# A fused spectral filter and ReGLU layer: the first chunk is split into halves behind an fp32 transpose, the opening list is rewritten, and the inverse pass copies its rows in steps of their own

## The chip, the cores and the metric

The kernel runs on one core of a Trainium2 chip. Its time is the device time of one execution in microseconds (us); the time of before is 449.02 us, the median of three runs (449.0 to 449.44).

## The reference, cut to what matters

```python
def reference(A_x, A_w_r, A_w_i, B_x, B_W_gate, B_W_up, B_W_down):   # x is (1, 2048, 448)
    x = A_x
    xn = _layernorm(x, axis=-1)
    X = rfft2(xn) * (w_r + 1j * w_i)            # over both axes, w is (2048, 225)
    y = irfft2(X)
    gate = xn @ W_gate                          # W_gate and W_up are (448, 1792)
    h = relu(gate) * (xn @ W_up)
    return x + y + h @ W_down                   # W_down is (1792, 448)
```

Both branches start from the same normalized rows and are added to the input.

## The kernel before, in words

Every fp32 operand of a matmul is split into two fp16 halves, a high one and a low one (the rounded value and the remainder), and a product takes three passes: high by high, low by high, high by low. The 2048 rows lie as 16 blocks of 128 rows. Block numbers go by `n2`; the four blocks with the same `n2 % 4` make a **chunk**, and the chunks are worked in the order 0, 2, 1, 3 (`CHUNKS`). A chunk's normalized rows are held transposed in a tile `T` (128 partitions x 8 slices x 512 columns: slices 0 to 3 the high halves of the 448 features, 4 to 6 and a part of 7 the low ones).

The gated branch is the bulk of TensorE's work. A unit `gu` (`gu_full`, L728 to L732) makes gate and up of one group of 128 hidden features for one chunk, in two banks of a PSUM tile `gu` of which there are two buffers. The 448 features don't fill four slices of 128, so the last half slices of two units are packed into four half-height matmuls (`gu_half`, L738) that stand together; the two units that share them are called mates. After a unit ScalarE takes relu of the gate (L768), VectorE multiplies (L772), ScalarE makes the high half (L776) and VectorE the low half (L780); only then is that `gu` buffer free. The down projection `dn` (L799) is added into `xy` by VectorE (L805). Hidden features go in groups of 5, 5 and 4.

The spectral branch runs behind this, as a list of background pieces (`bg`) that the scheduler hands out by a credit: column transforms by matmul (L361, L398, L630, L649), butterflies on VectorE (L404 to L428), the product with the filter (L502 to L505), and exchanges between the upper and the lower 64 partitions by DMA. In the inverse pass an exchange (`i_swap`, L591 to L593) first copies one row of a small tile `row` into partition 64 of the block's tile, which is a DMA issued on SyncE's queue (L592), and then issues two DMAs of 63 partitions into a tile `sw` (L529, L530); `i_pair` (L535, L536) adds the exchanged halves and `i_quad` (L602 to L607) makes sums and differences of the groups. Step numbers in the list `il` (L948) say how many steps after a block's exchange each piece comes: pair and quad stand at 2, `i_hi` at 3.

The first chunk's opening is an order written out by hand (`OPENING`, L30 to L41), one word for each piece, and within one engine the instructions stand in the order of these words. `lx` loads a block, `st` takes its mean and variance on VectorE, `sq` and `rs` make the reciprocal deviation (ScalarE, then four or five small VectorE instructions), `hi` writes the fp16 high half straight from the input on ScalarE (L300), `xn` the fp32 normalized rows on VectorE (L293), `lo` their difference (L317, L318), `cp` copies the odd columns on GpSimd. `tpA` and `tpB` are fp16 transposes on TensorE (L332), three of the high half and five of the rest for each block, into a PSUM tile `fx`, and `ev` copies them to `T` on VectorE (L340) or ScalarE (L338). `wsq`, `par`, `wsc`, `whi`, `wlo` scale and split the gate and up weights of one hidden group; `hh`, `lh`, `hl` are pieces of the first unit, over half of the chunk's columns each (the last digit names the half: 0 is blocks 0 and 4, 1 is blocks 8 and 12). `warm` and `kw1`, `kw3`, `kw6` are 19, 1, 3 and 6 matmuls on a tile of zeros whose result nobody reads (L1049). The later chunks are transposed by DMA (L326).

Of the kernel before, what the change touches and what calls it, by code (L numbers as in the profile page):

```python
# [9 lines left out]
F16 = mybir.dt.float16  # L10
# [20 lines left out]
lx0 lx4 lw lid lw lx8 lx12 lw lw lw lw lx2 lx10 lx6 lx14 lwd0 lwd1 lwd2 lwd3 lwd4 warm st0 st4 sqA rsA hi4  # L31
xn4 xn0 wsqW0g0 cp4 st8 hi0 parW0g0 st12 wsqW0g1 cp0 tpA0 lo0 tpA4 kw1 wscW0g0 sqB tpB0 kw6 parW0g1 wsqW1g0
rsB whiW0g0 vevB0 lo4 wsqW1g1 xn12 tpB4 kw3 hi8 parW1 wscW0g1 xn8 whiW0g1 cp8 vevA0 vevA4 hi12 tpA8 vevB4
hh10 hh00 lo8 wsqW2g1 cp12 tpA12 hl00 lo12 aevA12 tpB8 aevA8 hl10 wloW0g0 lw aevB8 tpB12 wscW1 lh00 aevB12
wloW0g1 lw lfd hh01 hh11 whiW1g0 st2 lh01 lh10 whiW1g1 hl01 wloW1g0 lw hl11 wsqW2g0 wloW1g1 lw ly0 ly4 ly8
ly12 lh11 wsqW3g0 st10 parW2 hp0 st14 wsqW3g1 gu1g0 st6 wdq0 parW3 wscW2 sqC wscW3 whiW2g0 rsC gu1g1 re0
wloW2g0 whiW3g1 tm0 whiW2g1 xn6 wsqW4g0 xn2 gu2g0 wloW2g1 hi2 re1 xn10 gh0 wloW3g1 whiW3g0 tm1 gu2g1 wdq1
wloW3g0 hi10 xn14 lo2 hi14 hi6 cp14 hp2 wsqW4g1 cp2 lo6 gu3g0 cp10 dm2 lo14 re2 parW4 wdq2 cp6 wscW4 tm2
whiW4g0 dm14 lo10 wdq4 gu3g1 wloW4g0 gh1 dm10 gl0 whiW4g1 gl1 dm6 gu4g0 re3 wloW4g1 wdq3 tm3 wdp gh3
wdsc gh2 gu4g1 gl2 wdh1 wdh2 wdl1 wdh0 wdl2 hp4 gl3 re4 wdh3 tm4 wdl0 gh4 wdh4 gl4 wdl3 wdl4  # L40
# [42 lines left out]
def _constants():  # L83
# [55 lines left out]
    ident = np.eye(128, dtype=np.float16)  # L139
# [5 lines left out]
def tile_gfnet_reglu(ctx: ExitStack, tc: tile.TileContext, x, xr, wgu, wd, wf, ident, c_fd, c_fm, c_im, c_row, c_id,  # L145
# [59 lines left out]
    id_t = ft([128, 128], F16, "id_t")  # L205
# [49 lines left out]
    rst = {}  # L255
# [7 lines left out]
    def ln_rstd(q, js=(0, 1, 2, 3), bias=False):  # L263
        w, m = rst[q, js[0]]
        sd, r0, t, r, nm = (w[:, i] for i in range(5))
        V.reciprocal(r0, sd)
        V.scalar_tensor_tensor(t, m[:, :, 1], 1e-5, r0, op0=OP.add, op1=OP.mult)
        V.scalar_tensor_tensor(t, t, -0.5 * 2048, r0, op0=OP.mult, op1=OP.mult)
        V.scalar_tensor_tensor(r, t, 1.5 * 2048, r0, op0=OP.add, op1=OP.mult)
        if bias:  # L270
            V.scalar_tensor_tensor(nm, m[:, :, 0], -1.0, r, op0=OP.mult, op1=OP.mult)
        for i, j in enumerate(js):
            rst[q, j] = r[:, i:i + 1], nm[:, i:i + 1], m[:, i, 0:1]
# [3 lines left out]
    for t in tts:  # L277
        G.memset(t[:, 7, 48:64], 0.0)
    for q in CHUNKS:
        G.memset(Tl[q][32:64], 0.0)  # L280

# [4 lines left out]
    def ln_xn(n2, act=False):  # L286
        xn_b[n2] = free.pop(0)
        xn[n2] = xn_b[n2].rearrange("p g c k -> p (g c k)")[:, 0:D]
        r, nm, mean = rst[n2 % 4, n2 // 4]
# [38 lines left out]
    def ln_tp(n2, tiles):  # L328
        if n2 not in tp:
            tp[n2] = fx().bitcast(F16).rearrange("p (a b) -> p a b", b=128)  # L330
        for a in tiles:
            P.transpose(tp[n2][:, a, :], tt[n2][:, a, :], id_t)  # L332

    def ln_ev(n2, a0, a1, act):
        q, j = n2 % 4, n2 // 4
        o = Tq[q][:, a0:a1, 128 * j:128 * (j + 1)]
        if act:
            last["A"] = A.activation(o, tp[n2][:, a0:a1], AF.Copy).ins  # L338
        else:
            last["V"] = V.tensor_copy(o, tp[n2][:, a0:a1]).ins  # L340


    def t_ninth(q):

        T = Tq[q]
        with tc.issue_after(last.get("R", last["S"])):
            for r in range(3):
                nc.sync.dma_start(Tl[q][16 * r:16 * (r + 1)], T[112:128, 4 + r])
            nc.sync.dma_start(Tl[q][64:128], T[64:128, 3])
# [867 lines left out]
```

## Time and profile before

| what | value |
|---|---|
| median of three runs | 449.02 us |
| profiled execution, its own time | 449.44 us |
| its span, first to last instruction | 447.6 us |
| TensorE busy / VectorE busy / ScalarE busy | 437.9 / 387.2 / 186.7 us |
| granted TensorE clock, mean of the span | 0.998 |

The profiled execution is the slowest of the three, 0.42 us above their median; 1.8 us of it lie outside the span. In a row of the timeline the first number is the start, the second the time from the first start to the last end of a group, and `x6` says how many instructions were merged; the square bracket holds the idle time before the group and what ended it. Matmuls are pipelined: the distance from start to start is what one costs the engine, while its own duration also holds the way through the array.

### The profile page before, as it was taken

Reading aid. Unit: us, or ns where it says so; the run is one execution under the profiler, and the core shown is the slowest. Engines: PE = TensorE matmul, PEld = TensorE weight load, DVE = VectorE, ACT = ScalarE, POOL = GpSimd, SP = SyncE. Lnnn points to the kernel's source line nnn. Section 1 sums busy time; section 2 is a strip of 40 time slices with the busy share of each in tenths; the row PEclk is TensorE's granted clock in tenths of the full one; section 3 lists DMA queues with packets and bytes.
Section 4 is the critical chain, followed back from the end, with each engine's and each line's share of the span. In section 5 each row is a group of like instructions: output and inputs, shape, how many; then the busy total and the mean of one; then the engine's idle time right before and its main releaser. Section 6 shows DMA issues by size and latency. Waiting matters only on the chain.

```text
span 447.6 us, 7353 instructions
## 1 busy us (share of the span) xinstructions
PE 437.9 (98%) x2616; PEld 218.8 (49%) x2616; DVE 387.2 (87%) x958; ACT 186.7 (42%) x398; POOL 28.8 (6%) x77
## 2 busy tenths in 40 slices
PE   6999999999999999999999999999999999999996
PEld 2644645545445444444444444444445555555653
DVE  5999779777969998999999999999789799699753
ACT  5896263742553955133124255344214134134230
POOL 4220020200100140000000000000000000000000
PEclk9999999999999999999999999999999999999999
DMA  7828985400001272412220210001011211211212
GB/s 259 313 68 246 320 334 105 96 0 22 2 1 48 95 243 74 132 54 72 84 84 2 83 41 1 1 1 61 23 41 55 68 34 56 89 34 48 94 63 82
DMA packets 37756, 39.54 MB, mean 88 GB/s; under 512 B 16550, under 2 KB 33624, under 8 KB 37720
## 3 DMA queue, kind: packets, MB, share of 16 engines
q1 hardware_dynamic: 37720, 39.09, 28.0%
q8 instruction: 20, 0.33, 0.3%
q14 instruction: 16, 0.13, 0.1%
HBM read 24.38 MB, written 3.67 MB: 63 GB/s over the span
## 4 chain that ended last, share of the span: by engine, by line
PE 52%; DVE 38%; DMA 3%; issue 3%; ACT 2%; POOL 1%; SPq 1%; DVEq 0%; ACTq 0%; POOLq 0%
PE gu L731 26%; PE dn L799 12%; DVE g L772 3%; DVE h L780 3%; DVE wt L685 3%; DVE xy L805 2%; PE fx L630 2%; PE fx L649 2%; DVE y L502 2%; DVE y L503 2%; DVE y L405 2%; DVE y L404 2%; DMA sw<-y 2%; DVE y L427 2%; PE gu L738 2%
## 5 line engine op out<-in xcount | busy, mean ns | idle before, releaser
L731 PE MATMUL gu<-T,wt 128*128 128x512 f16 (+1 forms) x1140 | 255.0, 375 | 0.0
L731 PEld LDWEIGHTS <-wt 128*128 128x128 f16 x1140 | 108.8, 98 | 128.3 <-issue 8.5
L799 PE MATMUL dn<-wdt,h 128*128 128x448 f16 x624 | 127.1, 352 | 0.3 <-DVE xy L805 0.3
L799 PEld LDWEIGHTS <-h 128*128 128x128 f16 x624 | 60.3, 98 | 57.7 <-issue 1.1
L776 ACT ACTIVATE h<-g 128x512 f16<-128x512 f32 x56 | 35.0, 627 | 78.8 <-DVE g L772 78.6
L768 ACT ACTIVATE g<-gu 128x512 f32<-128x512 f32 x56 | 33.0, 589 | 73.7 <-PE gu L738 52.1
L772 DVE SCALAR_TENSOR_TENSOR g<-gu,g 128x512 f32<-128x512 f32 x56 | 38.2, 682 | 4.2 <-ACT g L768 4.2
L780 DVE TENSOR_TENSOR h<-g,h 128x512 f16<-128x512 f32 x56 | 38.2, 683 | 3.1 <-ACT h L776 2.6
L805 DVE SCALAR_TENSOR_TENSOR xy<-dn,dsc,xy 128x448 f32<-128x448 f32 x44 | 29.8, 678 | 6.2 <-PE dn L799 6.2
L614 ACT ACTIVATE vt<-y,fsc 128x456 f16<-128x456 f32 x16 | 10.8, 672 | 29.9 <-PE fx L630 17.4
L681 ACT ACTIVATE wt<-wst,wsc 128x512 f16<-128x512 f32 x28 | 19.0, 714 | 6.2 <-DVE wsc L196 6.2
L189 POOL PARTITION_ALL_REDUCE wm<-wm x15 | 9.3, 617 | 181.9 <-ACT junk L186 161.8
L654 DVE SCALAR_TENSOR_TENSOR xy<-fx,fsc,xy 128x448 f32<-128x448 f32 x16 | 10.9, 679 | 11.0 <-PE fx L649 10.9
L685 DVE SCALAR_TENSOR_TENSOR wt<-wst,wsc,wt 128x512 f16<-128x512 f32 x28 | 20.2, 744 | 0.1
L738 PE MATMUL gu<-T,wt 64*128 64x512 f16 x112 | 17.0, 381 | 1.6 <-DVE g L772 1.4
L535 DVE TENSOR_TENSOR y<-y,sw 128x228 f32<-128x228 f32 x32 | 12.4, 388 | 6.8 <-DMA sw<-y 4.1
L186 ACT ACTIVATE junk<-wst 128x512 bf16<-128x512 f32 x28 | 17.4, 622 | 1.3 <-DMA wst<-in_wgu 1.0
L405 DVE TENSOR_TENSOR y<-y,y 128x456 f32<-128x456 f32 x22 | 13.8, 628 | 1.7 <-DMA row<-y 1.4
L392 DVE TENSOR_TENSOR Xh<-X,Xh 128x456 f16<-128x456 f32 x16 | 9.9, 626 | 5.8 <-ACT Xh L389 5.7
L404 DVE TENSOR_TENSOR y<-y,y 128x456 f32<-128x456 f32 x22 | 13.8, 628 | 0.4
L630 PE MATMUL fx<-im,vt 128*128 128x128 f16 x192 | 13.5, 219 | 0.0
L389 ACT ACTIVATE Xh<-X 128x456 f16<-128x456 f32 x16 | 9.2, 577 | 10.1 <-DVE X L387 8.9
(128 smaller groups left out, 476.2 us busy)
## 6 DMA issues: line engine op xcount, KB each, us to landing
sw<-y SPq DMA_DIRECT2D x64, 112.2 KB
wst<-in_wgu SPq DMA_DIRECT2D x28, 256.0 KB
wf<-in_wf SPq DMA_DIRECT2D x16, 228.0 KB
y<-in_xr SPq DMA_DIRECT2D x16, 224.0 KB
xy<-in_x SPq DMA_DIRECT2D x16, 224.0 KB
out<-xy SPq DMA_DIRECT2D x15, 224.0 KB
wdst<-in_wd SPq DMA_DIRECT2D x14, 224.0 KB
fm<-in_c_fm SPq DMA_DIRECT2D x4, 256.0 KB
```

What stands on the lines that cost most here:

```text
L404: V.tensor_tensor(t, a, b, op=OP.add)
L405: V.tensor_tensor(b, a, b, op=OP.subtract)
L630: P.matmul(o, v[:, h, w], m[:, c, :], start=(i == 0), stop=(i == 2), skip_group_check=True)
L685: V.scalar_tensor_tensor(w[:, 4:8, :], st, sc, w[:, 0:4, :], op0=OP.mult, op1=OP.subtract)
L731: last["P"] = P.matmul(hps[f, q][:, g, cs], wt[f, g][:, a, :], Tq[q][:, b, cs], start=(start and i == 0), stop=(stop and i == len(seq) - 1 ...
L738: m = P.matmul(hps[f, q][:, g, 0:512], wt[f, g][rows, 7, :], Tq[q][rows, b, :], start=start, stop=not start).ins
L768: last["A"] = A.activation(g1s[f, q], hps[f, q][:, 0, :], AF.Relu, scale=2.0 ** -22).ins
L772: last["V"] = V.scalar_tensor_tensor(g1, hps[f, q][:, 1, :], 2.0 ** -22, g1, op0=OP.mult, op1=OP.mult).ins
L776: A.activation(ht[f, q][:, 0, :], g1s[f, q], AF.Copy)
L780: V.tensor_tensor(h[:, 1, :], g1s.pop((f, q)), h[:, 0, :], op=OP.subtract)
L799: last["P"] = P.matmul(ps[:, 0:D], ht[f, q][:, a, js], wdt[f][:, b, :], start=(i == 0), stop=(i == n - 1)).ins
L805: last["V"] = V.scalar_tensor_tensor(xy[:, n2, :], dps[n2][:, 0:D], dsc[:, g:g + 1], xy[:, n2, :], op0=OP.mult, op1=OP.add).ins
```

## The change

The first chunk is no longer split before it is transposed. `ln_xw` (VectorE) writes the normalized fp32 rows of a block into the memory of its `tt` tile, `ln_xd` (ScalarE) doubles the last 64 columns, and `ln_tp` makes four transposes of 128 x 128 in fp32 with an fp32 identity (64 KB, loaded now from ScalarE's queue). `ln_thi` on ScalarE takes the high half out of PSUM in two instructions (64 rows of the last slice, then all four slices), and `ln_tlo` on VectorE subtracts it from PSUM for the low half, also in two. So 32 fp16 transposes become 16 in fp32, and `hi`, `xn`, `lo`, `cp` and `ev` of this chunk go. GpSimd clears one more piece of 32 x 512 before the tile of zeros is cleared, and the four small clears of `tt` move behind the transposes; `t_ninth` issues three more DMAs for this chunk.

The list `OPENING` is rewritten, with `rs` and `wsc` cut into single steps. The gate and up weights lie in memory with each 256 KB tile in one piece. In the inverse pass the row copy becomes a piece of its own, `i_row`, two steps after the exchange; `i_quad` goes from step 2 to step 3, all later pieces go one step later, and `stage4` is called one pair of blocks ahead, in the forward product too.

```diff
-lx0 lx4 lw lid lw lx8 lx12 lw lw lw lw lx2 lx10 lx6 lx14 lwd0 lwd1 lwd2 lwd3 lwd4 warm st0 st4 sqA rsA hi4
-xn4 xn0 wsqW0g0 cp4 st8 hi0 parW0g0 st12 wsqW0g1 cp0 tpA0 lo0 tpA4 kw1 wscW0g0 sqB tpB0 kw6 parW0g1 wsqW1g0
...
+lx0 lx4 lw st0 lx8 lx12 lw lw lw lwd2 lid lw lw lwd0 st4 lwd1
+lx6 root lx2 sqA lwd3 warm rsA0 rsA1 kw1 rsA2 rsA3 rsA4 wsqW0g0 lwd4 xn0 parW0g0
+xn4 xd0 xd4 tp0 wsqW0g1 tp4 st8 wscW0g0.0 parW0g1 st12 lx10 wscW0g0.1 lx14 sqB kw6 rsB0
+rsB1 wsqW1g0 whiW0g0 rsB2 rsB3 rsB4 tu0 kw3 th0 tu4 xn12 th4 xn8 tl0 tv0 wscW0g1.0
+xd12 wscW0g1.1 tv4 xd8 tl4 wloW0g0 wsqW1g1 hh00 whiW0g1 parW1 tp8 wscW1.0 wsqW2g1 tp12 tu12 lh00
+wloW0g1 wscW1.1 th12 lw hh10 tu8 hl10 tv12 tl12 th8 hl00 tl8 tv8 hh01 ly0 whiW1g1
...
-        eng.dma_start(wst[f, g], wgu[f, :, g])
+        eng.dma_start(wst[f, g], wgu[f, g])
...
-    for t in tts:
-        G.memset(t[:, 7, 48:64], 0.0)
     for q in CHUNKS:
         G.memset(Tl[q][32:64], 0.0)
+    G.memset(Tq[CHUNKS[0]][32:64, 7], 0.0)
...
+    def ln_xw(n2, act=False):
+        r, nm, mean = rn[n2 % 4, n2 // 4]
+        if act:
+            A.activation(xw[n2][:, 0:D], xr_t[n2], AF.Identity, scale=r, bias=nm)
+        else:
+            V.tensor_scalar(xw[n2][:, 0:D], xr_t[n2], mean, r, op0=OP.subtract, op1=OP.mult)
+
+    def ln_xd(n2):
+        A.activation(xw[n2][:, 448:512], xw[n2][:, 384:448], AF.Copy)
+
+    def ln_tp(n2):
+        tp[n2] = fx().rearrange("p (a b) -> p a b", b=128)
+        for a in range(4):
+            P.transpose(tp[n2][:, a, :], xw[n2][:, 128 * a:128 * (a + 1)], id_t)
+        G.memset(tts[n2 // 4][:, 7, 48:64], 0.0)
+
+    def ln_thi(n2, part):
+        q, j = n2 % 4, n2 // 4
+        T, js = Tq[q], slice(128 * j, 128 * (j + 1))
+        if part == 0:
+            A.activation(T[:, 0:4, js], tp[n2], AF.Copy)
+        else:
+            last["A"] = A.activation(T[64:128, 7, js], tp[n2][64:128, 3], AF.Copy).ins
+
+    def ln_tlo(n2, part):
+        q, j = n2 % 4, n2 // 4
+        T, js = Tq[q], slice(128 * j, 128 * (j + 1))
+        if part == 0:
+            V.tensor_tensor(T[:, 4:7, js], tp[n2][:, 0:3], T[:, 0:3, js], op=OP.subtract)
+        else:
+            last["V"] = V.tensor_tensor(T[64:128, 3, js], tp[n2][64:128, 3], T[64:128, 7, js], op=OP.subtract).ins
...
     def i_swap(n2):
-        nc.sync.dma_start(cur["U", n2][64:65], row[n2:n2 + 1])
         swap(("U", n2))
+    def i_row(n2):
+        nc.sync.dma_start(cur["U", n2][64:65], row[n2:n2 + 1])
...
+    add(bf[ks[0]], stage4, ks[0], 1, "s3", "X")
     for i0 in range(10):
         if i0 < 8:
             k0 = ks[i0]
             for k in (k0, k0 + 8):
                 add(0.0, load_wf, k)
-            add(bf[k0], stage4, k0, 1, "s3", "X")
+        if i0 < 7:
+            add(bf[ks[i0 + 1]], stage4, ks[i0 + 1], 1, "s3", "X")
...
-    il = ((8, 0.68, i_acc), (6, 0.0, i_pq), (4, 0.69, i_lo), (6, 0.69, i_pqlo), (2, 0.78, i_pair), (2, 1.83, i_quad),
-          (7, 0.0, i_ddft), (5, 0.0, i_sdft), (3, 0.0, i_hi), (0, 0.0, i_swap))
+    il = ((9, 0.68, i_acc), (7, 0.0, i_pq), (5, 0.69, i_lo), (7, 0.69, i_pqlo), (3, 1.83, i_quad), (2, 0.78, i_pair),
+          (8, 0.0, i_ddft), (6, 0.0, i_sdft), (4, 0.0, i_hi), (0, 0.0, i_swap), (2, 0.0, i_row))
```

**ScalarE in the opening.** The piece of ScalarE's order that feeds the second half of the chunk, before (`fx` with a number is a PSUM tile of one block, `junk` the output of the squares of a weight tile, `wt` a weight's high half):

```order
L186 ACTIVATE junk_235,wm_234<-wst_131 128x512
L681 ACTIVATE wt_242<-wst_124,wsc_217 128x512
L186 ACTIVATE junk_247,wm_234<-wst_133 128x512
L300 ACTIVATE tt2_105<-y2_72,rs_220 128x448
L681 ACTIVATE wt_264<-wst_127,wsc_260 128x512
L300 ACTIVATE tt3_106<-y3_73,rs_220 128x448
L186 ACTIVATE junk_285,wm_284<-wst_137 128x512
L338 ACTIVATE T0_62<-fx_289 128x3x128
L338 ACTIVATE T0_62<-fx_271 128x3x128
L338 ACTIVATE T0_62<-fx_271 128x5x128
L338 ACTIVATE T0_62<-fx_289 128x5x128
```

and after the change (`fx_190`, `fx_198`, `fx_271`, `fx_261` are blocks 0, 4, 12 and 8):

```order
L356 ACTIVATE T0_62<-fx_190 64x128
L354 ACTIVATE T0_62<-fx_190 128x4x128
L356 ACTIVATE T0_62<-fx_198 64x128
L354 ACTIVATE T0_62<-fx_198 128x4x128
L342 ACTIVATE tt3_106<-tt3_106 128x64
L342 ACTIVATE tt2_105<-tt2_105 128x64
L190 ACTIVATE junk_253,wm_226<-wst_131 128x512
L710 ACTIVATE wt_258<-wst_127,wsc_247 128x512
L190 ACTIVATE junk_269,wm_268<-wst_138 128x512
L356 ACTIVATE T0_62<-fx_271 64x128
L354 ACTIVATE T0_62<-fx_271 128x4x128
L356 ACTIVATE T0_62<-fx_261 64x128
```

The copies of blocks 8 and 12 still stand behind the squares and one weight's high half, but all four blocks are copied by ScalarE now, in two instructions each.

**TensorE between the second and the third group.** The mates `gu_3234` and `gu_3255` of before are the same two units as `gu_3215` and `gu_3236` of after; `wt` are their weights, `dn` and `h` belong to the down projection. Before:

```order
L731 MATMUL gu_3234<-T3_65,wt_2013 128x512
L738 LDWEIGHTS wt_2094
L738 MATMUL gu_3255<-T3_65,wt_2094 128x512
L738 LDWEIGHTS wt_2089
L738 MATMUL gu_3255<-T3_65,wt_2089 128x512
L738 LDWEIGHTS wt_2013
L738 MATMUL gu_3234<-T3_65,wt_2013 128x512
L738 LDWEIGHTS wt_2008
L738 MATMUL gu_3234<-T3_65,wt_2008 128x512
L799 LDWEIGHTS h_2820
L799 MATMUL dn_3192<-wdt_2198,h_2820 128x448
```

After:

```order
L828 MATMUL dn_3192<-wdt_2451,h_3079 128x448
L767 LDWEIGHTS wt_2065
L767 MATMUL gu_3236<-T3_65,wt_2065 128x512
L767 LDWEIGHTS wt_2060
L767 MATMUL gu_3236<-T3_65,wt_2060 128x512
L767 LDWEIGHTS wt_1986
L767 MATMUL gu_3215<-T3_65,wt_1986 128x512
L767 LDWEIGHTS wt_1981
L767 MATMUL gu_3215<-T3_65,wt_1981 128x512
L760 LDWEIGHTS wt_2060
L760 MATMUL gu_3236<-T3_65,wt_2060 128x512
```

Before, the four half-height matmuls close the first mate and 30 matmuls of the down projection follow; after, the 30 stand ahead of the four, and the second mate's 20 full matmuls follow at once.

At the same place on VectorE, the last rows ahead of the product that frees the buffer of `gu_3215` (`wt<-wst` is the low half of a weight, `y` and `wf` belong to the spectral product), after the change:

```order
L196 TENSOR_SCALAR eg_92<-wm_3062 128x2
L528 TENSOR_TENSOR y7_77<-y7_77,wf_2891 128x456
L200 TENSOR_SCALAR wsc_3248<-eg_92 128x2
L834 SCALAR_TENSOR_TENSOR xy_61<-dn_3192,dsc_94,xy_61 128x448
L196 TENSOR_SCALAR eg_92<-wm_3105 128x2
L529 TENSOR_TENSOR y13_83<-y13_83,y7_77 128x4x57
L530 TENSOR_TENSOR y13_83<-y13_83,y7_77 128x4x57
L200 TENSOR_SCALAR wsc_3293<-eg_92 128x2
L714 SCALAR_TENSOR_TENSOR wt_3286<-wst_2063,wsc_3248,wt_3286 128x512
L429 TENSOR_TENSOR y7_77<-y2_72,y13_83 128x456
L714 SCALAR_TENSOR_TENSOR wt_3289<-wst_2068,wsc_3248,wt_3289 128x512
L801 SCALAR_TENSOR_TENSOR g1_3260<-gu_3215,g1_3260 128x512
```

The product of the unit ahead of it (`g1_3119<-gu_3057`) stands 33 rows earlier on VectorE: four rows of the down projection's sum, four low halves of weights, 11 spectral rows of 456 columns, eight of 228, four small ones, one row `h`, and itself. Before, the same two products stood 17 rows apart.

**SyncE in the inverse pass.** The first exchanges of the inverse pass (`sw` is an exchange tile, `y` a block's tile), before:

```order
L529 DMA sw3_1907<-y15_85 63x456
L530 DMA sw3_1907<-y15_85 63x456
L592 DMA y7_77<-row_89 1x12x38
L592 DMA y9_79<-row_89 1x12x38
L592 DMA y5_75<-row_89 1x12x38
L592 DMA y15_85<-row_89 1x12x38
L592 DMA y4_74<-row_89 1x12x38
L529 DMA sw0_1904<-y4_74 63x456
L530 DMA sw0_1904<-y4_74 63x456
L592 DMA y10_80<-row_89 1x12x38
```

After:

```order
L554 DMA sw3_1888<-y11_81 63x456
L555 DMA sw3_1888<-y11_81 63x456
L620 DMA y7_77<-row_89 1x12x38
L554 DMA sw0_1885<-y4_74 63x456
L555 DMA sw0_1885<-y4_74 63x456
L620 DMA y13_83<-row_89 1x12x38
L554 DMA sw1_1886<-y16_86 63x456
L555 DMA sw1_1886<-y16_86 63x456
L620 DMA y5_75<-row_89 1x12x38
L554 DMA sw2_1887<-y12_82 63x456
```

Before, five row copies stand in one piece between the exchange of one block and that of the next; after, one row copy stands between two exchanges, and it belongs to a block that was exchanged four blocks earlier.

More of the change, by code (lines that the diff above doesn't have):

```diff
@@ L1085, in tile_gfnet_reglu @@
         piece(f"parW{f}", w_sum, f)
-        piece(f"wscW{f}", w_scale, f)
+        for k in range(2):
+            piece(f"wscW{f}.{k}", w_scale, f, (0, 1), k)
         for tag, fn in (("re", gu_relu), ("tm", gu_times), ("gh", gu_hi), ("gl", gu_lo)):
@@ L1097, in tile_gfnet_reglu @@
                 piece(f"parW{f}g{g}", w_sum, f, (g,))
-                piece(f"wscW{f}g{g}", w_scale, f, (g,))
+                for k in range(2):
+                    piece(f"wscW{f}g{g}.{k}", w_scale, f, (g,), k)
                 for h in range(2):
```

109 lines of the change are left out of this document (53 added, 56 removed).

## The prediction

> **What bounds the kernel now.** The head of the page comes first, then the waits of TensorE, then the window in which VectorE is fullest.
>
> ```profile
> span 447.6 us, 7353 instructions
> PE 437.9 (98%) x2616; PEld 218.8 (49%) x2616; DVE 387.2 (87%) x958; ACT 186.7 (42%) x398; POOL 28.8 (6%) x77
> ```
>
> ```profile
> PE dn L1049 <- POOL warm L1106: 3.6, 1, 3.6
> PE gu L738 <- DVE g L772: 1.4, 1, 1.4
> PE fx L332 <- ACT wt L681: 0.4, 1, 0.4
> PE dn L799 <- DVE xy L805: 0.3, 1, 0.3
> PE gu L738 <- DVE wt L685: 0.2, 1, 0.2
> ```
>
> ```profile
> 200.00:300.00 100.00, 100.00 (x496) 45.65 (x494) 98.06 (x214) 37.00 (x88) 3.21 (x5) 1.00 0.14 43
> ```
>
> TensorE is the bound. After its first matmul it waits five times, 5.9 us with the first, and 3.6 of these lie ahead of everything. A page of "busy" alone would not prove it, but here the starts follow each other at the pace of the matmuls from 14 us to the end. So the time is the TensorE work plus what stands ahead of it, plus its few waits, plus the tail. VectorE is the second bound: in the window from 200 to 300 us it is busy 98.06 of 100 us with 214 instructions. Work moved there shows at once.
>
> **The opening.** These are TensorE's rows of the opening, and GpSimd's, which release it.
>
> ```profile
> 3.58 6.97 PE L1049 MATMUL dn<-warm 128*128 128x512 f16 x19 [3.58 <-POOL warm L1106]
> 10.38 0.50 PE L332 MATMUL fx<-id_t,tt 128*128 128x128 f16 x6
> ...
> 10.93 0.44 PE L332 MATMUL fx<-id_t,tt 128*128 128x128 f16 x5
> 11.21 1.46 PE L1049 MATMUL dn<-warm 128*128 128x512 f16 x6
> ...
> 14.21 0.81 PE L731 MATMUL gu<-T,wt 128*128 128x256 f16 x6
> ...
> 16.54 3.01 PE L731 MATMUL gu<-T,wt 128*128 128x256 f16 x26
> 19.73 0.61 PE L738 MATMUL gu<-T,wt 64*128 64x512 f16 x4 [0.18 <-DVE wt L685]
> ```
>
> ```profile
> 0.74 0.24 POOL L278 MEMSET tt<- 128x16 f16 x4 [0.29 <-POOLq L1205]
> 1.03 1.90 POOL L280 MEMSET Tl<- 32x512 f16 x4
> 2.99 0.53 POOL L1106 MEMSET warm<- 128x512 f16 x1
> ```
>
> ```profile
> 6.19 0.93 DVE L293 TENSOR_SCALAR y<-y,mv,rs 128x448 f32<-128x448 f32 x2
> ```
>
> The four small clears ahead of the tile of zeros go (0.29 us, from 0.74 to 1.03), one of 32 x 512 comes ((2.99 - 1.03) / 4 = 0.49). TensorE starts 0.20 later, at 3.78. The 19 idle matmuls take 6.80 (3.58 to 10.38) and a twentieth one 0.22, so the first fp32 transpose stands at 10.80. The input it needs is long there: VectorE had the first two blocks' fp32 rows ready at 7.12 (6.19 + 0.93). So neither the order of the loads nor the identity's 64 KB on another queue costs anything up to some 3 us of delay; the identity's issue lies in idle time of ScalarE ahead of its first square root.
>
> From here the price T of one fp32 transpose decides. No row shows one. An fp16 transpose costs 0.056 (five from 10.93 to 11.21). A 512-column matmul, which streams as many columns as four passes of 128, costs 0.217 (six in 1.30 from 11.21 to 12.51). On top of these stands a weight load that may not hide:
>
> ```profile
> L332 PEld LDWEIGHTS <-tt 128*128 128x128 f16 x32 | 2.3, 98 | 1.6 <-ACT wt L681 0.9 <-DVE tt L317 0.2
> ```
>
> T is between 0.056 and 0.32 (0.22 + 0.098). I take 0.11, twice the fp16 price for twice the bytes, which is also near the 98 ns of one weight load.
>
> The Trainium skill differs with itself here. "FP8 and Floating Point Precision", section "TensorE Precision Notes", says that true fp32 makes four passes through the array, by which T would be 0.22; "TensorE: Matmul & The Clock Gate", section "Terms", lists a transpose mode on trn2 that is four times faster for fp32, by which T would be about 0.06. No row of before shows which holds, and my sum stands on neither.
>
> Eight transposes end at 10.80 + 8T = 11.68, nine idle matmuls (9 x 0.217 = 1.95) at 13.63. There the first gate matmul stands, against 14.21. Now ScalarE:
>
> ```profile
> 10.62 0.61 ACT L186 ACTIVATE junk<-wst 128x512 bf16<-128x512 f32 x1
> ...
> 15.23 0.49 ACT L338 ACTIVATE T<-fx 128x384 f16<-128x384 f16 x1
> ...
> 22.80 0.58 ACT L768 ACTIVATE g<-gu 128x512 f32<-128x512 f32 x1
> ```
>
> The first block leaves TensorE at 11.4. A copy of 512 columns out of PSUM is like the 0.58 of relu, 0.50 apart; the one of 64 rows and 128 columns, below the 0.49 for 384, I put at 0.2. Two blocks take 1.4 and are there at 12.9, ahead of 13.63. Then the two doublings (0.2 each), a square, a weight's high half and a square (0.62 each) and two blocks more: 12.8 + 0.4 + 1.86 + 1.4 + 0.1 = 16.55. TensorE has 17 half-width matmuls (0.107 each: 26 in 2.8 from 16.54) and eight transposes until it needs the second half, at 13.63 + 1.84 + 0.88 = 16.35. It waits some 0.2; as every row of that ScalarE chain is an estimate, I take 0.4. The other 23 matmuls take 2.48, and the four half-height ones stand at 19.2 against 19.73: **-0.5**. With T = 0.056 the wait grows to 0.8 and the sum is -0.9; with 0.22 it is +0.9; with 0.32, +2.5.
>
> Free: the cut `rs` and `wsc` steps (the same instructions), the weights in one piece (2 KB a row as before, and no wait for them), and the three more DMAs for the ninth slice, some 1.9 us of SyncE's issue. The last of that slice was issued here, and first read there:
>
> ```profile
> 41.41 0.59 SPq L349 DMA_DIRECT2D Tl<-T  x1
> ...
> 48.34 0.72 PE L361 MATMUL fx<-fd_t,T 128*128 128x114 f16 x11
> ```
>
> 1.9 us later, with the 2.3 us that a small copy takes below, is 46.2; if that cover were gone, TensorE would wait with its column transforms, which the matmuls of the down projection stand behind.
>
> **The inverse pass.** VectorE, SyncE and TensorE around the waits of 1.4 and 0.3:
>
> ```profile
> 315.92 0.40 DVE L535 TENSOR_TENSOR y<-y,sw 128x228 f32<-128x228 f32 x1 [2.65 <-DMA y<-row]
> ...
> 329.45 0.40 DVE L535 TENSOR_TENSOR y<-y,sw 128x228 f32<-128x228 f32 x1 [1.42 <-DMA sw<-y]
> ```
>
> ```profile
> 313.61 12.22 SPq L592 DMA_DIRECT2D y<-row  x5
> ```
>
> ```profile
> 336.16 0.61 PE L738 MATMUL gu<-T,wt 64*128 64x512 f16 x4 [1.40 <-DVE g L772]
> ```
>
> VectorE stands still 2.65 us for a row copy, issued at 313.61 and there at 315.9, and 1.42 for an exchange, because five row copies hold SyncE's queue for 12.22 us while each waits for its block. With the exchange first, the pair no longer waits for the row, and the row has a step until the sums of the quad. Both waits of VectorE should go, and with them TensorE's two: **-1.7**. The new wait is SyncE's: a row copy waits until the pair has been written, and the next block's exchange is queued behind it. That exchange has two steps, some 4 us, until its own pair; its landing takes about as long as those 2.3 us.
>
> What is late next? `stage4` comes one pair earlier, and the scheduler has laid the instructions anew. The costly place is between the second and third hidden group:
>
> ```profile
> 275.28 4.48 PE L731 MATMUL gu<-T,wt 128*128 128x512 f16 x20
> 279.69 0.60 PE L738 MATMUL gu<-T,wt 64*128 64x512 f16 x4
> 280.23 5.85 PE L799 MATMUL dn<-wdt,h 128*128 128x448 f16 x30
> 285.92 8.80 PE L731 MATMUL gu<-T,wt 128*128 128x512 f16 x40
> ```
>
> ```profile
> 275.64 0.68 DVE L772 SCALAR_TENSOR_TENSOR g<-gu,g 128x512 f32<-128x512 f32 x1
> 276.25 0.39 DVE L504 TENSOR_TENSOR y<-y,y 128x228 f32<-128x228 f32 x1
> ```
>
> ```profile
> L805 DVE SCALAR_TENSOR_TENSOR xy<-dn,dsc,xy 128x448 f32<-128x448 f32 x44 | 29.8, 678 | 6.2 <-PE dn L799 6.2
> L685 DVE SCALAR_TENSOR_TENSOR wt<-wst,wsc,wt 128x512 f16<-128x512 f32 x28 | 20.2, 744 | 0.1
> L502 DVE TENSOR_TENSOR y<-y,wf 128x456 f32<-128x456 f32 x16 | 10.1, 629 | 0.3
> ```
>
> Before, the first mate was complete at 280.2 and VectorE had 30 matmuls of time to free its buffer. After, its four half-height matmuls stand behind these 30, and the unit that takes its buffer follows 26 matmuls later: 275.28 + 4.41 + 5.69 + 0.54 + 4.41 (20 more) + 1.14 (six `dn` at 0.19) = 291.5. VectorE reaches the product that frees it 33 rows after the one of 275.64. By kind these are six rows of 0.68, four of 0.744, 11 of 0.63, eight of 0.39 and four small ones, which I put at 0.16, 17.7 us; by the window's pace (100 / 214 = 0.467) they are 15.4, because a row that needs nothing of the one ahead starts 0.07 before its end, as at 276.25. Half of them do need it: 16.2. The product ends at 275.64 + 16.2 + 0.68 = 292.5, a wait of **+1.0**; the bounds are 0.2 (15.4) and 2.5 (17.7).
>
> **The tail.** All later pieces of the inverse pass go one step later.
>
> ```profile
> 437.54 0.75 PE L649 MATMUL fx<-idc_t,pgh 114*128 114x112 f16 x12
> 438.13 1.11 PE L818 MATMUL dn<-wdt,h 128*128 128x448 f16 x5
> ```
>
> Five matmuls (some 1 us, then the first `fx` of the tail) stood behind the last transform; in the new order none does, and the tail's first `fx` tile is freed only when VectorE has added the transform before it, 0.2 + 0.68 after its end, of which the last transform covers 0.59: **+0.3**.
>
> **The sum.** -0.5 - 1.7 + 1.0 + 0.3 = -0.9, against the profiled execution's 449.44 (span 447.6 and 1.8 around it): 448.5. That execution lies 0.42 above the median of 449.02, so the forecast for a median is 448.1.
>
> **The rivals.**
> - *The transposes cost one weight load and four passes, none of it hidden* (T = 0.32). The opening is then +2.5 and the time 449.02 + 2.1 = 451.1. It turns to slower by 0.9 from T = 0.25 on (16 transposes, nearly all on the path once ScalarE no longer covers them). For it: weight load and matmul are one instruction in the new program, where fp16 has two. Against it: an fp16 load of 98 ns hides behind matmuls of 56.
> - *Four passes, loads hidden* (T = 0.22): +0.5, 449.5. This is what the Trainium skill's page on precision gives, in the sentence above.
> - *VectorE's lateness moves but does not shrink*: the waits of 1.7 come back at 291 us and beside it in full, and the kernel gains the opening less the tail, 448.8. For it: 98.06 of 100 us.
> - *A cheap transpose and no new wait* (T = 0.056, 15.4 us for the 33 rows): -0.9 - 1.7 + 0.2 + 0.3 = -2.1, 446.9.
> - That the change doesn't do what it says is unlikely: its orders show each piece in its place.
>
> **How the numbers follow.** Forecast 0.40, of which 0.28 faster and 0.12 within the bound; cheap transpose 0.13, faster; lateness moved 0.15 (0.12 same, 0.03 slower); four passes hidden 0.12 (0.09 same, 0.03 slower); four passes and loads 0.20, slower. A change of 0.2%, 0.9 us, is about what a measurement of this kernel can tell from none. Faster 0.41, same 0.33, slower 0.26. The range runs from the cheap case, 446.8, to short of the dear one, 450.7; the forecast's own is 447.3 to 449.2.
>
> **What would show it.** The fp32 transposes' distance from start to start gives T. The first gate matmul should stand at 13.6, the half-height ones at 19.2; the waits of VectorE for `y<-row` and for `sw<-y` at 329 should be gone; TensorE should wait about 1.0 near 291 for VectorE's product and 0.3 near 438. I am wrong if T is above 0.25, if ScalarE's copies hold the second half back by more than a microsecond, or if VectorE's product at 291 is on time.

## The result: 450.07 us, 0.2% slower, where 448.1 and 0.2% faster was forecast

The changed kernel takes 450.07 us (median of 16 runs, 449.45 to 450.97), before 449.33 (16 runs on the same chip): a ratio of 1.002, 95% interval 1.0012 to 1.0028. The sign is wrong. The profiled execution took 449.82 us.

The head of its page:

```profile
span 448.0 us, 7327 instructions
PE 437.8 (98%) x2600; PEld 218.2 (49%) x2600; DVE 387.2 (86%) x955; ACT 185.0 (41%) x402; POOL 28.8 (6%) x70
```

TensorE and VectorE have the same work as before (437.9 and 387.2 us), so the difference lies in waits and in the pace of the first matmuls. TensorE's waits (engine, line, what it waited for; total, times, longest):

```profile
PE dn L1082 <- POOL warm L1140: 3.7, 1, 3.7
PE gu L760 <- DVE g L801: 1.4, 3, 0.9
PE fx L347 <- DVE T L362: 0.4, 1, 0.4
PE dn L828 <- ACT h L805: 0.4, 1, 0.4
PE gu L760 <- ACT T L354: 0.3, 1, 0.3
PE fx L847 <- DVE xy L681: 0.2, 1, 0.2
```

The waits of 1.4 and 0.3 of before are gone, as forecast. In their place stand one of 0.9, also forecast, and several of 0.2 to 0.4; of these only the one for ScalarE's copies (`T L354`) and the one of the tail (`xy L681`) were forecast. TensorE's rows of the opening:

```profile
3.75 5.85 PE L1082 MATMUL dn<-warm 128*128 128x512 f16 x20 [3.75 <-POOL warm L1140]
9.43 1.04 PE L347 MATMUL fx<-id_t,tt 128*128 128x128 f32 x8
10.31 2.10 PE L1082 MATMUL dn<-warm 128*128 128x512 f16 x9
12.43 0.49 PE L760 MATMUL gu<-T,wt 128*128 128x256 f16 x3
12.76 0.60 PE L347 MATMUL fx<-id_t,tt 128*128 128x128 f32 x4
13.79 0.63 PE L347 MATMUL fx<-id_t,tt 128*128 128x128 f32 x4 [0.43 <-DVE T L362]
14.36 1.70 PE L760 MATMUL gu<-T,wt 128*128 128x256 f16 x14
16.37 2.67 PE L760 MATMUL gu<-T,wt 128*128 128x256 f16 x23 [0.31 <-ACT T L354]
18.97 0.61 PE L767 MATMUL gu<-T,wt 64*128 64x512 f16 x4
19.51 4.49 PE L760 MATMUL gu<-T,wt 128*128 128x512 f16 x20
24.19 4.48 PE L760 MATMUL gu<-T,wt 128*128 128x512 f16 x20 [0.19 <-DVE g L801]
```

Eight fp32 transposes take 10.31 - 9.43 = 0.88: **T is 0.11**, as taken. But the 20 idle matmuls take 5.68 (3.75 to 9.43), where before 19 took 6.80. They begin at half pace (0.427 apart instead of 0.216), and that stretch was seven matmuls long here and 13 before. So this execution's half-height matmuls, 0.76 earlier than in before, were helped by the pace and are no measure of the opening. The experiments sort that out.

Three places behind the opening, TensorE's rows:

```profile
260.11 1.87 PE L828 MATMUL dn<-wdt,h 128*128 128x448 f16 x9
262.26 2.10 PE L760 MATMUL gu<-T,wt 128*128 128x512 f16 x9 [0.28 <-DVE g L801]
```

```profile
271.53 1.87 PE L828 MATMUL dn<-wdt,h 128*128 128x448 f16 x9
273.79 2.64 PE L828 MATMUL dn<-wdt,h 128*128 128x448 f16 x12 [0.39 <-ACT h L805]
```

```profile
291.22 1.30 PE L828 MATMUL dn<-wdt,h 128*128 128x448 f16 x6
293.46 1.89 PE L760 MATMUL gu<-T,wt 128*128 128x512 f16 x8 [0.94 <-DVE g L801]
```

The bracket counts idle time after the modelled end of the last matmul; from start to start the losses are larger. Nine `dn` at 0.19 from 260.11 end at 261.8, the next start is 0.45 later; at 273.8 it is 0.56, at 293.5 it is 1.1, and at 24.2 (20 matmuls at 0.216 from 19.51) 0.36.

At 262 the bracket names VectorE, but VectorE itself stood still. ScalarE's rows, then VectorE's:

```profile
260.70 0.30 ACT L521 ACTIVATE wf<-wf 128x114 f32<-128x114 f32 x1 [11.19 <-DMA wf<-in_wf]
260.90 0.58 ACT L797 ACTIVATE g<-gu 128x512 f32<-128x512 f32 x1
```

```profile
261.52 0.69 DVE L801 SCALAR_TENSOR_TENSOR g<-gu,g 128x512 f32<-128x512 f32 x1 [0.94 <-ACT g L797]
```

The relu stood on ScalarE behind a step of the product with the filter, which waited for the load of `wf`. SyncE issued that load at 257.50, behind exchanges that had waited for VectorE until 254.38. In before the load went out at 251.88 and the relu stood at 256.69. At 273 VectorE's own order is late: the relu was ready at 268.3, and VectorE, without standing still, came to the product at 272.39.

At 293 it is VectorE's order again. The relu of the unit, then VectorE's product ahead of it and its own:

```profile
290.88 0.58 ACT L797 ACTIVATE g<-gu 128x512 f32<-128x512 f32 x1
```

```profile
276.69 0.68 DVE L801 SCALAR_TENSOR_TENSOR g<-gu,g 128x512 f32<-128x512 f32 x1
...
292.72 0.68 DVE L801 SCALAR_TENSOR_TENSOR g<-gu,g 128x512 f32<-128x512 f32 x1
```

The relu was ready at 291.46. VectorE does not stand still between 265 and 293; it comes to the product, 33 rows behind the one ahead of it, after 16.03 us (276.69 to 292.72), where 16.2 was forecast. It is this product that frees the `gu` buffer: the two halves of `h`, made behind it, are read from `g` and not from PSUM.

### The profile page after: what moved, and what is told of

It is laid out like the page before. It is cut to its first block, busy times and chain, and to the rows that moved or that the text cites. A ratio compares the mean times of both kernels' runs of the same rounds, so it can differ in the third digit from the quotient of the medians.

```text
span 448.0 us, 7327 instructions
## 1 busy us (share of the span) xinstructions
PE 437.8 (98%) x2600; PEld 218.2 (49%) x2600; DVE 387.2 (86%) x955; ACT 185.0 (41%) x402; POOL 28.8 (6%) x70
## 4 chain that ended last, share of the span: by engine, by line
PE 64%; DVE 26%; DMA 3%; ACT 2%; issue 2%; SPq 1%; DVEq 0%; ACTq 0%
PE gu L760 35%; PE dn L828 16%; PE fx L657 2%; PE fx L386 2%; PE gu L767 2%; DVE g L801 2%; PE fx L423 2%; PE fx L676 2%; DVE y L527 2%; DVE xy L834 2%; DVE y L429 2%; DVE y L528 2%; DVE h L809 2%; DVE y L430 2%; DVE y L452 1%
## 5 line engine op out<-in xcount | busy, mean ns | idle before, releaser
L681 DVE SCALAR_TENSOR_TENSOR xy<-fx,fsc,xy 128x448 f32<-128x448 f32 x16 | 10.8, 682 | 7.9 <-PE fx L676 7.7
L521 ACT ACTIVATE wf<-wf 128x114 f32<-128x114 f32 x16 | 4.4, 292 | 23.2 <-DMA wf<-in_wf 21.8
L742 ACT ACTIVATE wdt<-wdst,wds 128x448 f16<-128x448 f32 x14 | 8.9, 659 | 10.6 <-PE dn L828 7.0
```

## The experiments

Short names: O is the new opening, F the call of `stage4` one pair ahead in the forward product, I the edits of the inverse pass. The changed kernel is O + F + I. Each ratio is taken against before in the same set of runs, where its median was 449.04 to 449.33.

### Taking the three parts apart

`opening_alone` (O): the changed kernel without F and I.

```diff
-    il = ((9, 0.68, i_acc), ... (3, 1.83, i_quad), ... (2, 0.0, i_row))
+    il = ((8, 0.68, i_acc), ... (2, 1.83, i_quad), ... (0, 0.0, i_swap))
-    add(bf[ks[0]], stage4, ks[0], 1, "s3", "X")
...
-            add(bf[ks[i0 + 1]], stage4, ks[i0 + 1], 1, "s3", "X")
+            add(bf[k0], stage4, k0, 1, "s3", "X")
```

> The changed kernel with both passes of the spectral branch as they were before: the row copy inside the exchange, quad at step 2, stage4 not ahead. What is left is the opening. Theory M (my main one: the opening gains, the new waits at 262 to 292 us in the spectral product lose): TensorE's waits of 1.7 near 319 and 335 us return, none stands between 262 and 292, and the time is before less 0.5, ratio 0.999. Theory O (the opening only looks good because the clock rose 2.4 us earlier in the profiled execution, 6 half-speed matmuls instead of 12; on average it loses): 0.5 above before, ratio 1.001.

Measured: 452.13 us, ratio 1.0061 (1.0044 to 1.0078). Both theories fell: O loses 3 us, not 0.5. The loss stands behind the opening: from start to start TensorE's waits behind 20 us add up to 5.0 us in its trace (1.65 ahead of 195 us and 1.63 ahead of 323 among them), those of before to 1.8.

`inverse_alone` (F + I): before with the same edits the other way round.

> Before, with only the edits of the spectral branch: row copy as a step of its own, quad at step 3, stage4 one pair ahead in both passes. Theory M: waits of some 1.9 in all at 262 to 292 us, no waits at 319 and 335 (1.7 gone), 0.3 more in the tail: 0.5 slower than before, ratio 1.001. Theory O (the spectral branch is at worst even, the loss is the opening's): 0 to 0.5 faster than before, ratio 0.999 to 1.000.

Measured: 450.33 us, 1.0023 (1.0014 to 1.0032). Theory M's direction; a wait of 1.0 stands at 293.76.

`product_back` (O + I): only the `stage4` lines of the forward product go back.

> The changed kernel with stage4 of the forward product called where it was before; the inverse pass stays changed. Theory M with the forward lookahead as the cause: the waits at 262, 273 and 292 us (0.45, 0.55, 1.10 from start to start over the usual distance) go and nothing comes for them: 1.9 less than the changed kernel, 448.2, ratio to before 0.997. Theory D (VectorE is full there and the lateness only moves): the waits come back at another unit, the time stays within 0.5 of the changed kernel, ratio 1.001 to 1.003.

Measured: 450.75 us, 1.0034 (1.0021 to 1.0047). The waits at 262 and 293 went, but others came (0.6 near 193 and 0.2 near 227, both for products of VectorE), and that of 0.4 near 275 stayed. That is theory D's side, a little beyond its range. The trace is that of the fastest of its five runs (449.44).

`inverse_back` (O + F): only the lines of the inverse pass go back.

> The changed kernel with the inverse pass as before (row copy in the exchange, quad at step 2, stage4 not ahead there); the forward product stays one pair ahead. Theory M: the waits at 262 to 292 us stay (1.9), those of 1.7 near 319 and 335 come back, the 0.3 of the tail goes: 1.4 slower than the changed kernel, ratio 1.005. Theory D: VectorE's lateness at 292 us is part of the same backlog that shows at 319 and 335, so the two don't add: within 0.5 of the changed kernel, ratio 1.001 to 1.003.

Measured: 451.29 us, 1.0043 (1.0031 to 1.0055), 1.2 above the changed kernel (1.0 by the ratios), nearer to M's 1.4 than to D's 0.5.

`inverse_pass_only` (I): before with `i_row`, the new `il` and the inverse pass's `stage4` lines, nothing else.

> Before with the edits of the inverse pass alone (row copy as its own step, quad at step 3, its stage4 one pair ahead); the forward product's stage4 stays where it was, and so does the opening. In the runs so far a wait of 1.1 near 292 us stands in each kernel with the forward lookahead and in none without, one of 0.8 to 1.65 near 193 us only in the new opening without it, those near 320 and 335 only with the old inverse pass. Theory M2 (each wait belongs to its edit): none of the three here, 0.35 in the tail: before less 1.5, 447.7, ratio 0.997. Rival D (VectorE's lateness only moves): new waits of 1 or more somewhere between 190 and 340, ratio 0.999 to 1.003.

Measured: **447.68 us, 0.9965** (0.9954 to 0.9976), M2's number, and the fastest kernel of this study. TensorE's waits in it:

```profile
...
PE fx L332 <- ACT wt L683: 0.5, 1, 0.5
PE fx L820 <- DVE xy L656: 0.2, 1, 0.2
PE gu L740 <- DVE wt L687: 0.2, 1, 0.2
```

None of 0.2 or more is left between the opening and the tail.

`product_ahead_only` (F): before with the forward product's `stage4` lines.

> Before with only stage4 of the forward product called one pair ahead; opening and inverse pass stay. Theory M2 (the edit has its own price): TensorE's waits near 266 and 292 us come on top of before's two at 319 and 335: the difference of the two kernels with the changed inverse pass, 450.33 - 447.68 = 2.65, on 449.3: 451.9, ratio 1.006. Theory V (the waits are VectorE's backlog in the stretch where it is full; time lost at 292 is not lost again at 335): 0.5 to 1.5 above before, ratio 1.001 to 1.003.

Measured: 449.56 us, 1.0006 (0.9997 to 1.0015): no difference that can be told. Theory V was nearer (0.5). Its waits of TensorE, and one of VectorE:

```profile
...
PE gu L731 <- DVE g L772: 1.0, 1, 1.0
...
PE gu L738 <- DVE g L772: 0.3, 1, 0.3
```

```profile
DVE y L535 <- DMA y<-row: 2.0, 1, 2.0
```

VectorE still stands 2.0 us for a row copy, but TensorE's wait of 1.4 at 336 is gone: TensorE has lost its time already near 266 and 292 and comes 2 us later to the four half-height matmuls near 320 (321.04, in before 319.07), and VectorE is ready.

| parts | us | ratio |
|---|---|---|
| O | 452.13 | 1.0061 |
| F | 449.56 | 1.0006 |
| I | 447.68 | 0.9965 |
| F + I | 450.33 | 1.0023 |
| O + I | 450.75 | 1.0034 |
| O + F | 451.29 | 1.0043 |
| O + F + I | 450.07 | 1.0020 |

The parts don't add: O, F and I alone sum to 1.0032. With the old opening F costs next to nothing beside the old inverse pass and 2.6 us (450.33 - 447.68) beside the new one; with the new opening it takes 0.7 to 0.8 off the medians, though the intervals overlap there. O costs some 3 us alone and beside I, 1.7 beside F, and nothing that can be told with F and I (450.07 against 450.33).

### The wait at 293 us

`halves_first`: the unit whose half-height matmuls fell behind the 30 of the down projection moves up two places in the list of units.

```diff
     units += pend
+    i = units.index(gseq[36])
+    units.insert(i - 2, units.pop(i))
```

> The changed kernel, with the unit between the second and third hidden group put two down projections earlier in the list of units, so that its four half-height matmuls stand ahead of the 30 of the down projection again, as in before. Theory M (the place of the four sets the wait near 292 us): the wait of 0.94 there goes, the time is 0.9 less than the changed kernel, ratio about 1.000. Theory V (VectorE has 3.7 us of work less behind it at 191 us than in before, and TensorE waits for it at the next place that offers itself): TensorE waits about as much in all between 190 and 345 us (2.3 in the changed kernel), at other units; the time stays within 0.4 of the changed kernel.

Measured: 448.82 us, 0.9998 (0.9989 to 1.0007), 1.0 less than the changed kernel by the ratios. Its rows at the place:

```profile
280.48 0.61 PE L767 MATMUL gu<-T,wt 64*128 64x512 f16 x4
281.02 5.85 PE L828 MATMUL dn<-wdt,h 128*128 128x448 f16 x30
286.71 8.80 PE L760 MATMUL gu<-T,wt 128*128 128x512 f16 x40
```

The four stand ahead of the 30, the 40 behind run through, and nothing of 0.3 or more came in its place behind them. VectorE's order moved with the unit: where 33 rows lay between two products there are now 18 and then 22 (products at 276.49, 285.44 and 295.60). So the order of the units makes the wait; the waits at 262 and 273 stayed.

`less_vector`: the changed kernel without one sum in the product with the filter; the imaginary part of that product is left incomplete.

```diff
-        V.tensor_tensor(t[:, :, 1], t[:, :, 1], xt[:, :, 0], op=OP.add)
```

> The changed kernel without the second sum of the product with the filter (L530, 16 rows of VectorE, 0.31 from start to start, 5.0 us between 170 and 300 us); the imaginary part of that product is left incomplete. The 30 matmuls still stand ahead of the four half-height ones. Theory V: VectorE is in time from about 240 us on, the waits at 262, 273, 292 shrink to nothing, 2.0 to 2.4 less than the changed kernel, ratio 0.997. Theory M: the order on TensorE is what makes the wait near 292 us; at least 0.5 of its 0.94 stays, 1.0 to 1.5 less than the changed kernel, ratio 0.999.

Measured: 449.63 us, 1.0007 (0.9998 to 1.0017). Two places of its trace:

```profile
250.74 0.60 PE L766 MATMUL gu<-T,wt 64*128 64x512 f16 x4
...
286.63 0.61 PE L766 MATMUL gu<-T,wt 64*128 64x512 f16 x4
...
291.50 1.30 PE L827 MATMUL dn<-wdt,h 128*128 128x448 f16 x6
293.62 4.48 PE L759 MATMUL gu<-T,wt 128*128 128x512 f16 x20 [0.82 <-DVE g L800]
```

0.82 of the 0.94 stays, but the run doesn't part the theories. The scheduler laid other spectral rows where the sums had been: between the two products stand 33 rows of VectorE again, and they take 16.55 us (276.34 to 292.89), so VectorE had no less to do there. The waits of 0.28 at 262 and 0.39 at 273 are gone, but TensorE's order is another one there too: the four half-height matmuls at 250.74 stand ahead of the 30 of the down projection, which in the changed kernel they follow (30 from 249.25, the four at 255.24). What made these two waits go is not shown. The time fell by 0.4 to 0.6 by the ratios, less than either theory had said; the profiled execution had the longest stretch at half pace of all (14 matmuls, gate at 13.76), which can explain its own time but not the median.

### The opening: pace, idle matmuls, VectorE

`after_again`: the changed kernel once more.

> The changed kernel once more, for a second profiled execution and a time beside the next three. Theory C (the moment at which TensorE's clock rises is drawn anew in each execution, and the changed opening passes it on until ScalarE bounds it): half-speed matmuls anywhere from 6 to 13, the first gate matmul at 12.4 to 13.6 accordingly, everything behind 24 us as in the first profile; ratio to before again 1.001 to 1.003. Theory P (the clock's rise belongs to the program): 6 half-speed matmuls and 12.43 again.

Measured: 449.86 us, 1.0015 (1.0006 to 1.0023), first gate matmul at 12.70 after nine matmuls at half pace: theory C. Over all profiles the stretch was 7 to 14 matmuls. With the new opening the gate stood at 12.43 after seven, 12.70 after nine, 13.23 after eleven, 13.63 after 13 (`opening_alone`):

```profile
3.75 7.23 PE L1076 MATMUL dn<-warm 128*128 128x512 f16 x20 [3.75 <-POOL warm L1134]
10.81 1.04 PE L347 MATMUL fx<-id_t,tt 128*128 128x128 f32 x8
11.69 2.10 PE L1076 MATMUL dn<-warm 128*128 128x512 f16 x9
13.63 0.49 PE L758 MATMUL gu<-T,wt 128*128 128x256 f16 x3
13.96 1.32 PE L347 MATMUL fx<-id_t,tt 128*128 128x128 f32 x8
15.21 1.70 PE L758 MATMUL gu<-T,wt 128*128 128x256 f16 x14
17.22 2.67 PE L758 MATMUL gu<-T,wt 128*128 128x256 f16 x23 [0.31 <-ACT T L354]
19.83 0.60 PE L765 MATMUL gu<-T,wt 64*128 64x512 f16 x4
```

Here the stretch is as long as in before: 13.63 to the digit of the forecast, but the half-height matmuls at 19.83, not 19.2.

`fewer_idle`: `kw6` and `kw3` go from the list.

```diff
-xn4 xd0 xd4 tp0 ... sqB kw6 rsB0
+xn4 xd0 xd4 tp0 ... sqB rsB0
-rsB1 wsqW1g0 whiW0g0 rsB2 rsB3 rsB4 tu0 kw3 th0 ...
+rsB1 wsqW1g0 whiW0g0 rsB2 rsB3 rsB4 tu0 th0 ...
```

> The changed kernel without the nine idle matmuls between the first transposes and the first gate matmul (1.94 us of TensorE at full clock). Theory C: they only fill TensorE's wait for ScalarE's copies when the clock rises early, and hold the gate matmul back when it rises late; without them the gate stands about 1.8 behind the first transpose, at 12.4 to 12.9, whatever the clock does: 0.3 to 0.6 less than the changed kernel on average, ratio 0.999 to 1.001 if the rest of the order stays. Rival I (the idle matmuls keep the clock up): after a pause of some 1.5 us the first gate matmuls run at half speed, 1 to 3 us slower than the changed kernel.

Measured: 450.69 us, 1.0032 (1.002 to 1.0044). The gate stood at 12.47, as C said, and then rival I struck. In the windows, the number behind POOL's count is the granted clock:

```profile
14.00:16.00 2.00, 2.00 (x12) 1.40 (x12) 1.57 (x6) 1.84 (x6) 0.11 (x1) 0.54 1.05 377
16.00:18.00 2.00, 2.00 (x13) 1.49 (x12) 1.89 (x4) 2.00 (x4) 0.00 (x0) 0.61 1.05 389
```

After a pause of 1.61 us and one of 0.43 TensorE ran at a granted clock of 0.5 for 3.41 us, from 14.16 on; 0.54 and 0.61 are the means of the two windows, which hold some full pace too.

`warm_first`: the tile of zeros is cleared ahead of the five clears of 32 x 512.

```diff
+    G.memset(warm, 0.0)
     for q in CHUNKS:
         G.memset(Tl[q][32:64], 0.0)
...
-        G.memset(warm, 0.0)
```

> The changed kernel with the tile of zeros cleared ahead of the five clears of 32 x 512: the idle matmuls start about 2.4 us earlier (near 1.3). Theory C: the 20 idle ones are over by 7 to 8.5 us, the transposes stand at about 8, the gate matmul at 12.4 where ScalarE's copies end, in every execution: 0.3 to 0.9 less than the changed kernel, ratio 0.999 to 1.001. Theory P or no effect of the clock: the same time as the changed kernel, because ScalarE bounds the gate at 12.4 already.

Measured: 449.66 us, 1.001 (1.0002 to 1.0019), gate at 12.36 although its stretch was 12 matmuls long. Against the changed kernel, which lay at 449.86 in the same set of runs, this is too little to tell. TensorE waited 1.28 there for ScalarE's copy: from about 12.4 on ScalarE bounds the gate.

`inverse_and_warm`: the same move of that clear in `inverse_pass_only`.

> Before with the edits of the inverse pass alone, as run already (447.68, ratio 0.9965), and with the tile of zeros cleared first on GpSimd, so that the idle matmuls start some 2.3 us earlier. Theory C (the late rise of the clock costs this opening too, since VectorE waited 0.6 for the transposes): 0.3 to 0.6 less than without, ratio 0.995 to 0.996. Rival: ScalarE and the loads bound this opening, the ratio stays at 0.9965.

Measured: 447.96 us, 0.9969 (0.9956 to 0.9981): the rival, no gain.

`weights_end_oi` and `weights_end_ofi`: O + I and O + F + I, with the last 22 words of the list in the order of before.

```diff
-re3 wloW4g1 tm3 wdsc wdh3 wdl3 wdh2 gu4g1 wdh4 wdh1 hp4 re4 wdl1 tm4 gh3 wdl2
-wdh0 gh2 gl3 gh4 wdl4 wdl0 gl2 gl4
+re3 wloW4g1 tm3 gh3 wdsc gh2 gu4g1 gl2 wdh1 wdh2 wdl1 wdh0 wdl2 hp4 gl3 re4 wdh3 tm4
+wdl0 gh4 wdh4 gl4 wdl3 wdl4
```

> The changed opening and the changed inverse pass, with stage4 of the forward product as before (450.75 as run), and the last 22 words of the opening list, which make the down weights and finish the units 1 to 4, put into the order that before has. In the trace VectorE waits there 0.7 and 1.0 for two high halves of down weights (near 38 and 39 us), then 3.6 for the down projection (2.4 in before). Theory V (VectorE is 2.7 us of work behind before at 191 us, and waits of TensorE between 190 and 345 us come from that): those 1.7 go, TensorE's waits near 193 and 274 shrink, 0.8 to 1.7 less, 449.0 to 450.0, ratio 1.000 to 1.002. Rival (the order further on is laid the same way and the waits stay): 450.5 to 450.9.

> The changed kernel itself with the same 22 words in the order of before. Theory V: the waits near 262 and 273 us shrink, that of 0.94 near 292 stays (it stands with the place of the four half-height matmuls, as the runs showed): 0.5 to 1.2 less, 448.9 to 449.5, ratio 0.999 to 1.000. Rival: the same 449.9 to 450.1.

Measured: 449.17 us, 0.9997 (0.9981 to 1.0012), 1.6 less than O + I; and 450.73 us, 1.0037 (1.0021 to 1.0052), 0.7 more than the changed kernel. The window from 24 to 190 us (TensorE, its weight loads, VectorE, ScalarE busy), for before, O + I, and O + I with the old end:

```profile
24.00:190.00 166.00, 166.00 (x964) 81.21 (x963) 141.93 (x373) 86.70 (x190) 17.88 (x45) 1.00 0.40 118
```

```profile
24.00:190.00 166.00, 165.81 (x962) 81.14 (x962) 137.97 (x368) 85.27 (x190) 18.60 (x45) 1.00 0.39 114
```

```profile
24.00:190.00 166.00, 165.81 (x962) 80.96 (x961) 141.42 (x372) 86.75 (x191) 17.84 (x45) 1.00 0.43 116
```

With the new opening VectorE does 4 us less in this stretch (137.97 for 141.93, of nearly the same total) and brings that work into the stretch from 190 us on, where it has little room (busy 150.09 of the 155 us to 345, in before 148.23). The old end of the list gives back 3.5 of it, and 1.6 of the time by the medians. That the one causes the other is argued, not shown: the profiled executions, 449.51 with the old end and 449.44 without, don't differ by those 1.6. Beside F it gives VectorE the same (141.52) and the kernel nothing: there TensorE waits 0.9 near 268 and 1.1 near 295 for products. For that kernel theory V failed, and why its order came out worse was not tried.

## Why the prediction was wrong, step by step

- **TensorE is the bound, VectorE the second.** Right, but weaker than the traces support: from 190 to 345 us either may set the time, so a wait taken away at one place may have been paid at another already (F beside the old inverse pass).
- **T = 0.11.** Right, 0.11 in 8 transposes and in all kernels with them. The estimates from the Trainium skill's two figures ("FP8 and Floating Point Precision", "TensorE Precision Notes": four passes; "TensorE: Matmul & The Clock Gate", "Terms": a mode four times faster) were 0.22 and 0.06; neither agrees with this trace. The weight load, which the first rival has in one instruction with the transpose, is a row of its own in the trace, and hidden.
- **The opening, -0.5.** Failed. The gate came at 13.63 as forecast where the half pace lasted as long, but 6.2 us lay between gate and half-height matmuls instead of 5.57. In `opening_alone` the second eight transposes took 1.25 (13.96 to 15.21) instead of 0.88, since the fourth block waited for a PSUM tile that VectorE still read (0.43 in the bracket of the changed kernel); the second half came 0.48 late (14 matmuls at 0.109 from 15.21 end at 16.74, the next start is 17.22) instead of 0.4; and 0.1 went at the change to the half-height matmuls. ScalarE's copies take 0.9 for a block (10.60 to 11.50 in the changed kernel), not 0.7. A wait of 0.36 at 24 us, for a product of VectorE, was not in the sum at all. With 13 matmuls at half pace the half-height ones stand at 19.83 against 19.73, with eleven at 19.43 (`inverse_back`) against 19.57 (`inverse_pass_only`), with nine at 18.90 against 19.33 (`product_ahead_only`). With the 0.36 on top the new opening is 0.5 worse, 0.2 worse and 0.1 better: it gains nothing on the mean.
- **The opening's length depends on the pace.** Not seen. I took the half pace of one execution for a constant.
- **The inverse pass, -1.7.** Right by itself: `inverse_pass_only` gains 1.6 with the tail's 0.3 in it, and in the changed kernel both waits of TensorE are gone, as are VectorE's for the row copy and for the exchange at 329.
- **"What is late next", +1.0 near 291.** The mechanism and its size were right (0.94, at the unit named, with 16.03 us for the 33 rows), and `halves_first` shows that the order of the units makes it. **The step that failed is that I called it the costly place and priced no other.** The waits at 262 and 273 us and two smaller ones near 204 and 275, some 1.4 from start to start, were left out, though the quoted window showed VectorE full through all of it. At 262 the way led over a load that SyncE issued late, which looking at VectorE's products alone would have missed.
- **The tail, +0.3.** Right, by these rows of the changed kernel:

```profile
438.17 1.34 PE L676 MATMUL fx<-idc_t,pgh 114*128 114x112 f16 x24
439.70 4.71 PE L847 MATMUL fx<-wdt,h 128*128 128x448 f16 x27 [0.19 <-DVE xy L681]
```

  Twelve such matmuls took 0.59 in before (437.54 to 438.13), 24 take 1.18; the next start is 0.35 later than that.
- **The sum.** With an opening between -0.1 and +0.5, -1.8 (the old waits from start to start), 1.1, 1.4 and 0.3, it is +0.9 to +1.5; measured was +0.74. (Old waits, from start to start beyond the usual step: 1.46 ahead of the row of 336.16, and 0.35 ahead of the 30 `dn` near 320.)
- **The rivals.** "VectorE's lateness moves but does not shrink" was the nearest, with 448.8 and a chance of 0.15. It lacked that VectorE gets later: I compared TensorE's openings and did not count what VectorE had done by the end of the list (138.42 us of work between 24 and 190 us in the changed kernel, 141.93 in before). How much of the loss this makes stays open, since giving the work back did not help the changed kernel (`weights_end_ofi`). All my rivals on the slow side hung on T. So the upper end of the range, 450.7, stood there for a reason that turned out not to hold.

What stays open besides: O still costs 1.5 us beside I with its old end (449.17 against 447.68), no run here splits that further, and no run takes away the waits at 262 and 273 alone.

## What to carry to other kernels

A change that lays a full second engine's instructions anew has to be priced by that engine's whole account: how much of its work is done when its full stretch begins, then every place where the first engine waits for it, not the one place that looks worst. Parts of a change that take away waits of the same two engines don't add; run each alone, since here the best kernel was one part of three. The order of the last 22 words of the opening list changed the median by 1.6 us beside I and by 0.7 the other way beside F + I, though TensorE waits for nothing there. And where a wait names an engine, look whether that engine itself stood still: at 262 us it did, and what was late was a load further up the chain.

## What the runs showed of the hardware

- TensorE's first matmuls run at half pace (0.427 for 512 columns instead of 0.216) for 7 to 14 matmuls, 2.9 to some 5.9 us, different from execution to execution, while the profile's column of the granted clock reads 1.00. The traces have no record of the clock ahead of its rise: in all 16 the first one begins within 0.15 us of the end of that stretch (at 6.54 us in the changed kernel, 9.07 in before), and what has no record is shown as 1.00. The Trainium skill ("TensorE: Matmul & The Clock Gate", "What's actually happening") says that the clock rises after a window of about 3.4 us that runs freely. The spread of 3 us fits such a window, but not the 0.5 us to either side that the section gives for it, and the shortest stretch, 2.9, is under one window.
- A pause of 1.61 us, with one of 0.43 behind it, was followed by 3.41 us at a granted clock of 0.5 (`fewer_idle`); pauses of 1.28 and 0.43 were not (`warm_first`). The same page of the Trainium skill, under "HAM oscillation", puts the limit for a pause at about 3.4 us; here it was less, in the one kernel that shows it. With the nine matmuls whose result nobody reads, 1.94 us of TensorE's time, the kernel was 0.8 us faster (449.86 against 450.69).
- A 128 x 128 transpose in fp32 costs 0.11 from start to start, twice one in fp16 (0.056). Each has a weight load of its own, 0.14 long in the trace against 0.098 for fp16, and it is hidden behind the transpose ahead.
